# Q of a linear-attention layer computed token by token and turned by the DMA crossbar, its last group computed later, two weights in one buffer

## The chip, the cores and the metric

The kernel runs on one core of a Trainium2 chip. That core has five instruction streams that run side by side and wait for one another by semaphores: PE (TensorE, matmuls; its weight loads are listed as PEld), ACT (ScalarE, activation functions), DVE (VectorE), POOL (GpSimd) and SP (SyncE, which here issues the DMAs). The metric is the device time of one execution in microseconds (us), lower is better. Matmul results go to PSUM, which is cut here into four slots of two banks; everything else lies in SBUF, 128 partitions wide.

## The reference

For x of 2048 tokens by 448 features, two branches work on the same normalised input and are summed with the residual:

```
xn = layernorm(x)
A: q,k,v = xn @ wqkv          16 heads of 28
   pq, pk = q @ w_phi, k @ w_phi (per head)
   phi(p) = [softmax(p), softmax(-p)]          56 features a head
   kv = phi_k^T @ v;  z = sum over tokens of phi_k
   A = ((phi_q @ kv) / (phi_q . z + 1e-6)) @ wo
B: h  = gelu(layernorm(xn) @ w1), its four column blocks shifted by 1, -1, 2, -2 tokens
   x1 = xn + h @ w2
   B  = x1 + gelu(layernorm(x1) @ w3) @ w4
out = x + A + B
```

## The kernel before

Tokens are cut into 16 tiles of 128 (NT), four groups of four tiles. 448 rows of contraction are 3.5 times 128, so nearly every product is done by `pair448` (line 710): two products side by side, each of seven 64-row matmuls, in two halves `.a` (8 matmuls) and `.b` (6); one call is a "pass" of 14 matmuls and takes one PSUM slot. Since the 64-row matmuls run in pairs, a pass costs seven pair steps.

Stages, in the order of data:

- Loads (lines 583 to 637) are issued by SP: x in six pieces, wk, wq, wv and w1, then, after the x transposes, w2 and its copy w2s (lines 1051 to 1056), w3, wo and w4 (lines 1102 to 1104).
- First norm: per tile `st` (statistics), `ag`, `sc` (a power on POOL), `ap` (apply), `du` (lines 762 to 782). xn is then transposed to xnT: tiles 0 to 3 by PE (`xT`, line 794), tiles 4 to 15 each by one DMA transpose on SP, 128x512, `xD4` to `xD15` (line 815).
- w_phi is folded into wk and wq, giving wpk and wpq (`wT`, `fold`, `foldc`, lines 825 to 872).
- `V0` to `V7` (line 890) and `K0` to `K7` (line 908) take a pair of tiles each, tokens on the partitions, 448 columns. K's result is exponentiated twice on ACT (`.e0`, `.e1`), summed per head on DVE (`red`, `rec`) and scaled mostly on POOL (`nrm`).
- `Q0` to `Q7` (line 942) take a group of four tiles and half of the head blocks each: features on the partitions (120), 512 columns of tokens, two exponentials of 120x1024 on ACT straight into eq, which is the stationary operand that `num` needs. Nothing has to be transposed.
- `W10` to `W17` (line 961): w1, with `gel` on ACT (32 instructions), writing each shifted block where it belongs; tiles at the seam go through `nudge` and `put` (lines 980 to 1001). `warm2` loads ACT's gelu table after all exponentials of K and Q.
- `hD0` to `hD7` (line 1002): DMA transposes on SP, 128x1024, of two tiles of h into hT, a ring of three buffers; `W20` to `W27` (line 1061) multiply hT by w2.
- `kv0` to `kv3`, `kvc`, `kvm`, `kvo` (lines 1014 to 1047) make the 56x29 matrix per head.
- Second norm per pair: `W2j.r`, `st2`, `ag2`, `sc2`, `ga`, and `gD` (line 1097), a DMA transpose of g into gT, which has two slots of four tiles.
- `H` (line 1185): w3 and gelu, seven passes of 512 columns a group. `num`, `n1` to `n7`, `od`, `oD` (lines 1110 to 1180): the attention output, normalised on DVE and POOL and transposed on SP. `F` (lines 1214 to 1236): w4 and wo for a pair of tiles, then `fin` on DVE and `out`, one each per tile (lines 1237 to 1247).

What order each engine's instructions have is settled before launch: a list scheduler (class Planner, line 223) starts tasks by a rank and by assumed durations (the third argument of `P.add`), and the table RANKS (line 366) overrides all ranks. Each engine then works strictly in that order, so an instruction that waits holds back all behind it on its engine; on SP that is every DMA issue. Waits are derived from the bytes that instructions touch (class Recorder, line 17), so two uses of one buffer wait for one another. All operations are recorded by helpers: L197 is every matmul, L201 every PE transpose, L205 every ACT instruction, L209 every elementwise one, L212 every plain DMA and L215 every DMA transpose. In the profile's names "eq" is also the buffer in which wk, wq lie at first, "hq" the buffer of h and at first of wpq, "w" any of w1, w2, w3, w4, "wv" also g, "phik" also the H activations, and "xnT<-xnT" is `oD`.

Of the kernel before, what the change touches and what calls it, by code (L numbers as in the profile page):

```python
# [366 lines left out]
warm 868.4 tiny 970.5 phi -70.0 x0 -486.0 x1 -79.6 wk0 -291.7 wk1 284.2 x2 326.9 wv0 1117.1 wv1 954.7 wv2 792.3 wq0  # L367
444.5 wq1 375.6 x4 733.3 x8 1139.7 x12 1546.2 w10 640.0 w11 1288.0 w12 1936.1 bdl -321.6 bdh 970.7@5139 mask
1098.4@1625 pick 966.2@4497 ident 958.1@1998 mhalf -318.4 z_h 959.3@1573 nudge 971.2@1597 z_pk -285.0 z_v -272.1 z_wpq
998.3 z_kvq 286.2 st0 853.0 ag0 208.4 sc0e 294.4 sc0 -285.3 ap0 258.7 du0 57.9 st1 204.5 ag1 60.2@4897 sc1e 288.1 sc1  # L370
997.3 ap1 243.1 du1 1112.4 st2 205.2 ag2 227.0 st3 252.9 ag3 294.2 sc2e 1063.7 sc2 970.7 ap2 63.9 ap3 271.9 du2 268.8
st4 84.4 ag4 239.6 st5 239.8 ag5 874.0 sc4e 102.1 sc4 991.8 ap4 286.4 ap5 495.5 du4 65.4 st6 287.4@11185 ag6 865.4 st7
239.4@11166 ag7 156.1 sc6e 205.0 sc6 971.2@13677 ap6 157.0 ap7 220.7 du6 90.4 st8 28.7@13523 ag8 243.2@16614 st9
288.9@13637 ag9 413.8 sc8e -323.1 sc8 1243.7 ap8 782.0@20130 ap9 797.1 du8 1090.5 st10 243.7@13806 ag10 84.0 st11
259.2@13643 ag11 205.1 sc10e 244.0 sc10 986.2 ap10 495.3 ap11 156.9 du10 82.0@20186 st12 313.5 ag12 204.3 st13 761.4
ag13 28.6@20784 sc12e 263.1 sc12 1162.8 ap12 176.8 ap13 157.2 du12 369.7 st14 234.9@18290 ag14 305.3@19922 st15
82.9@17719 ag15 228.5@19848 sc14e 313.4 sc14 1188.5@22933 ap14 251.2 ap15 262.1 du14 264.6 f0 1188.9 f8 870.9@24467
xT0 296.7@6540 xT1 589.9@8454 xTc0 769.9@7438 xTc1 829.3 xT2 308.9 xT3 575.0 xTc2 822.2@11260 xTc3 896.9@11975 xD4
463.2 xD5 487.3 xD6 397.4 xD7 480.3 xD8 479.7 xD9 456.4 xD10 490.4 xD11 488.2 xD12 476.1@27407 xD13 425.8@25657 xD14
422.8@28403 xD15 486.3@30159 wTk 278.3 wTck0 872.2 wTck1 847.2 foldk0 291.2@8902 foldck0 873.4 foldk1 290.8@7999  # L380
foldck1 861.1 wTq 597.2@7001 wTcq0 815.4 wTcq1 576.6 foldq0 112.7@9432 foldcq0 873.8@10814 foldq1 309.8 foldcq1
770.5@11650 V0.a 131.0 V0.b 596.4 V0.e 814.9 V1.a 611.2 V1.b 621.0 V1.e -217.9 V2.a 283.7@19412 V2.b 243.7 V2.e 855.1
V3.a 258.1@25132 V3.b 615.5 V3.e 530.1 V4.a 413.8 V4.b 487.7@32840 V4.e 648.6 V5.a 2130.9 V5.b 315.3 V5.e 343.8 V6.a
1092.4 V6.b 656.1 V6.e 491.9 V7.a 1096.5 V7.b 374.4 V7.e -228.4 K0.a 590.7 K0.b 596.7 K0.e0 875.6 K0.e1 507.0 red0
1501.6 rec0 1501.9 nrm0 1188.1 red1 1498.0@21181 rec1 118.3 nrm1 1157.5 K1.a 283.9@17349 K1.b 609.8 K1.e0 509.1 K1.e1
-216.6 red2 786.6 rec2 515.2 nrm2 1160.2 red3 264.5@32297 rec3 290.1 nrm3 1159.4 K2.a 575.7 K2.b 283.4 K2.e0
-202.6@23116 K2.e1 919.1 red4 797.0 rec4 226.8 nrm4 870.8 red5 1498.8 rec5 293.5 nrm5 407.5@40914 K3.a 183.0 K3.b
621.3 K3.e0 828.9 K3.e1 501.7 red6 1377.0 rec6 499.7 nrm6 399.9@33939 red7 516.5@30012 rec7 1379.7 nrm7 1187.7 K4.a
675.4 K4.b 1438.8 K4.e0 729.0 K4.e1 718.7 red8 1533.4 rec8 1413.5 nrm8 390.6 red9 1380.6 rec9 1474.4 nrm9 407.3 K5.a
644.7@37806 K5.b 683.8 K5.e0 496.9 K5.e1 496.4 red10 1439.5 rec10 -331.0 nrm10 403.0 red11 1435.2@50122 rec11  # L390
-297.4@53022 nrm11 415.4 K6.a 401.9 K6.b 644.6 K6.e0 -263.9@34806 K6.e1 501.3@33944 red12 1500.3 rec12 1437.9 nrm12
857.2 red13 1417.4 rec13 1380.5 nrm13 1159.5 K7.a 682.7 K7.b 1126.1 K7.e0 493.7 K7.e1 648.4 red14 307.4 rec14 1462.0
nrm14 1098.5 red15 1418.2 rec15 1474.5 nrm15 407.1 Q0.a 569.0 Q0.b 263.5 Q0.e0 543.6 Q0.e1 543.6 Q1.a 290.1 Q1.b 596.6
Q1.e0 785.1 Q1.e1 522.7 Q2.a 1491.2 Q2.b 261.5 Q2.e0 647.5@28961 Q2.e1 242.8@28196 Q3.a 595.2 Q3.b 242.4 Q3.e0 785.4
Q3.e1 -312.2 Q4.a 175.1 Q4.b 283.7 Q4.e0 904.2@33049 Q4.e1 498.8 Q5.a 355.3 Q5.b 413.2 Q5.e0 499.2 Q5.e1 903.8 Q6.a
594.9 Q6.b 478.9 Q6.e0 492.2 Q6.e1 529.8 Q7.a 1057.0 Q7.b 683.2 Q7.e0 349.0 Q7.e1 660.7 warm2 529.2@45117 W10.a
656.5@43897 W10.b 949.8 gel0.0 728.6 gel0.1 340.6 gel1.0 532.8 gel1.1 744.8 W11.a 804.7 W11.b 213.9 gel2.0 -228.0
gel2.1 658.3 gel3.0 482.7 gel3.1 659.0 W12.a 916.6 W12.b 930.6 gel4.0 349.8 gel4.1 494.5 gel5.0 519.7 gel5.1 482.9
W13.a 1439.6 W13.b 682.4 gel6.0 640.8 gel6.1 725.6 gel7.0 492.4@53544 gel7.1 493.3@52599 W14.a 1446.7 W14.b 1478.5
gel8.0 644.4 gel8.1 372.5 gel9.0 349.8@55542 gel9.1 494.5 W15.a 1073.7@51311 W15.b 525.8 gel10.0 658.6 gel10.1 656.9  # L400
gel11.0 349.9 gel11.1 350.4 W16.a 2141.1 W16.b 1086.0 gel12.0 358.7 gel12.1 492.6@57478 gel13.0 688.0 gel13.1
366.6@57534 W17.a 687.1 W17.b 707.4 gel14.0 491.3 gel14.1 492.1 gel15.0 366.1 gel15.1 -228.4 nudge0 1075.4@59991 put8
505.8@60597 put9 327.7@61558 nudge1 1073.1 put7 492.5 put6 736.9 hD0 177.9 hD1 147.9 hD2 187.5 hD3 194.4 hD4 213.9 hD5
223.0@59251 hD6 199.2 hD7 198.0@59683 kv0 918.8 kv1 1477.9 kv2 1071.3 kv3 882.5 kvc 1430.0 kvm 259.3 kvo0 1803.8 kvo1
1544.6 w20 485.1 w21 419.6 w22 417.3 w23 525.4 W20.a 1446.5 W20.b 1060.2 W20.r 1493.4 st2_0 1438.4 ag2_0 1431.6 st2_1
1535.3 ag2_1 1020.8@59199 sc2_0e 1487.3 sc2_0 409.9@61475 ga0 1036.1 ga1 1450.3@62958 gD0 187.6 W21.a 214.3 W21.b
523.9 W21.r 1464.6 st2_2 1438.2 ag2_2 1488.1 st2_3 1437.9 ag2_3 1464.8 sc2_2e 1556.8 sc2_2 376.0 ga2 1418.4 ga3 1036.5
gD1 162.3 W22.a 525.7 W22.b 525.6 W22.r 1557.2 st2_4 1535.7@63878 ag2_4 1826.3 st2_5 1750.8 ag2_5 909.6@73450 sc2_4e
1470.9@74052 sc2_4 947.9@75836 ga4 1547.5 ga5 1503.7 gD2 148.3 W23.a 497.9 W23.b 524.6 W23.r 1849.7 st2_6 1900.8 ag2_6
1451.3 st2_7 1813.2 ag2_7 1410.1@73193 sc2_6e 1487.6 sc2_6 857.8 ga6 1036.7 ga7 749.0 gD3 157.7 W24.a 297.4@76488  # L410
W24.b 525.9 W24.r 1874.5 st2_8 1416.0 ag2_8 1033.4 st2_9 1529.3 ag2_9 1721.7 sc2_8e 1548.2 sc2_8 666.0 ga8 743.9 ga9
1943.6 gD4 266.5@86330 W25.a 907.3 W25.b 279.2@65249 W25.r 1518.3@67862 st2_10 1906.4 ag2_10 1504.1 st2_11
1545.7@73156 ag2_11 1739.6@75171 sc2_10e 1901.7 sc2_10 872.0 ga10 1813.1 ga11 749.7@85280 gD5 290.3 W26.a 1070.4 W26.b
465.7@63251 W26.r 1813.1 st2_12 1567.0@67359 ag2_12 1825.8 st2_13 1036.4@66877 ag2_13 1885.8@74867 sc2_12e 1826.4
sc2_12 407.8 ga12 1828.6 ga13 1545.9@100527 gD6 1700.4 W27.a 283.9@66012 W27.b 297.5 W27.r 1503.5 st2_14 1419.6 ag2_14
1437.5@71900 st2_15 1825.9@74052 ag2_15 1548.0 sc2_14e 1548.2@82777 sc2_14 925.1 ga14 746.9@95166 ga15 1904.0 gD7
1685.8 w30 419.0 w31 406.5 wo0 423.1 wo1 491.3 wo2 461.4 w4 494.1 num0 466.2 n1_0 1546.3 n2_0 1393.7 n3_0 1760.0@76183
n4_0 749.2 n5_0 1904.7 n6_0 1069.2 n7_0 936.0 num1 525.7 n1_1 1544.5 n2_1 1896.2 n3_1 1470.5@81970 n4_1 1559.1 n5_1
1776.2 n6_1 1813.2 n7_1 927.9@86239 od0 1946.5 oD0 268.1 num2 504.3@83674 n1_2 1526.8@85094 n2_2 1770.0 n3_2 1039.2
n4_2 989.8 n5_2 1778.7 n6_2 1814.1 n7_2 1695.3 num3 541.1 n1_3 1796.4 n2_3 1722.5 n3_3 1957.9 n4_3 1527.3 n5_3 1001.0  # L420
n6_3 1526.9 n7_3 662.7 od1 1896.2 oD1 293.4 num4 551.0 n1_4 752.3 n2_4 1546.2 n3_4 1901.0 n4_4 748.0 n5_4 2206.7 n6_4
1533.1 n7_4 1772.9 num5 557.6 n1_5 751.8 n2_5 2205.0 n3_5 1021.6 n4_5 1512.8 n5_5 1021.8 n6_5 1596.5 n7_5 598.4 od2
1015.6 oD2 1674.3 num6 841.7 n1_6 1513.0 n2_6 723.9 n3_6 1593.5 n4_6 745.4 n5_6 1010.2 n6_6 1594.1 n7_6 663.6@106936
num7 1026.4 n1_7 2207.5 n2_7 1545.8 n3_7 1545.5 n4_7 2209.9 n5_7 744.5 n6_7 1542.2 n7_7 600.2 od3 1884.4 oD3 1734.2
# [29 lines left out]
def bass_parallel_sum__linear_kernel_hedgehog__mixer_s_mlp__prompt_kernel(  # L454
# [18 lines left out]
    with es:  # L473
# [62 lines left out]
        for nm, w in (("st", 6), ("mv", 2), ("rs", 2), ("fs", 4), ("st2", 6), ("mv2", 2), ("rs2", 2)):  # L536
            stat[nm] = new(nm, NT * w, F32).rearrange("p (t c) -> p t c", t=NT)
# [423 lines left out]
        for j in range(8):  # L961
# [5 lines left out]
            for d, i in enumerate((i0, i1)):  # L967
                for q in range(2):
# [7 lines left out]
                    for m in (2 * q, 2 * q + 1):  # L976
                        made[i, m] = g_
# [304 lines left out]
```

The softmax here doesn't subtract the row's maximum and nothing guards it: scores larger than these inputs give would overflow.

## Time and profile before

| | |
|---|---|
| time, median of 3 runs | 177.67 us (177.43 to 177.85) |
| the profiled execution | 177.84 us, its span 176.1 us |
| granted TensorE clock | 1.000 |
| longest idle of PE after its start | 0.93, 0.53, 0.43, 0.32 us |
| last matmul group starts, by the PE timeline | 172.82 us, `F7_1.b` |
| ACT_TABLE_LOAD | 2 of 1283 ns |
| exponential 128x896 (K), mean | 954 ns, x16 |
| exponential 120x1024 (Q), mean | 1061 ns, x16 |
| DMA transposes, issue to landing | xnT 2.5, hT 3.3, gT 3.3, oT 3.1 us |

The share of busy time is an average over stages. A PE that is shown as busy nearly all the time says that whatever is taken off PE's stream can shorten the kernel, and that whatever makes PE wait lengthens it; it does not say that the work is the least there could be. Durations of matmuls in a list are from issue to end and overlap: two neighbours of 349 ns start 0.19 us after the pair before. Cost is therefore read from the starts of groups in the timeline.

### The profile page before, as it was taken

What the parts mean: (1) busy time and instruction counts of PE and PEld (TensorE: products, weight loads), DVE (VectorE), ACT (ScalarE), POOL (GpSimd) and SP (SyncE); (2) the same over time, 40 slices, a digit from 0 to 9 for tenths busy, and PEclk for the clock granted to TensorE, in tenths of its full rate; (3) what the DMA queues carried; (4) which work ended last, traced back from release to release, by engine and by line L of the source; (5) the groups of instructions that cost most, each with busy time, mean ns of one, the idle gap of its engine ahead of it and who ended that gap; (6) DMA issues with size and microseconds to landing.
All of it is one profiled execution on the core that took longest, in us unless ns stands there. A gap on an engine that the chain in (4) does not pass through costs nothing.

```text
span 176.1 us, 4846 instructions
## 1 busy us (share of the span) xinstructions
PE 169.2 (96%) x2080; PEld 111.4 (63%) x2080; DVE 116.4 (66%) x300; ACT 81.4 (46%) x116; POOL 77.8 (44%) x105
## 2 busy tenths in 40 slices
PE   5999999999999979999999999999999999999993
PEld 4766566676666665455555667655676666766793
DVE  3879999977995798995986655830654554370133
ACT  3398999999999510264557100327001561200000
POOL 7515578699339334035432253640037141261080
PEclk9999999999999999999999999999999999999999
DMA  6993444599918496625054616130010403313022
GB/s 146 279 339 83 72 83 91 101 360 327 331 49 162 77 122 123 119 32 93 0 98 86 120 27 149 53 63 0 0 56 26 89 0 63 60 52 63 0 86 78
DMA packets 41766, 18.30 MB, mean 104 GB/s; under 512 B 33552, under 2 KB 40848, under 8 KB 41744
## 3 DMA queue, kind: packets, MB, share of 16 engines
q1 hardware_dynamic: 41136, 17.91, 43.2%
q8 instruction: 16, 0.26, 0.6%
q10 hardware_dynamic: 608, 0.08, 0.3%
q14 instruction: 6, 0.05, 0.1%
HBM read 8.28 MB, written 1.84 MB: 57 GB/s over the span
## 4 chain that ended last, share of the span: by engine, by line
PE 86%; DMA 8%; SPq 3%; issue 1%; DVE 0%; DVEq 0%
PE ps L197 86%; DMA wv<-in_A_wqkv_dram 4%; SPq L212 3%; DMA hT<-hq 3%; DMA gT<-wv 2%; DVE vaug L209 0%; DVEq L169 0%; SPq L215 0%
## 5 line engine op out<-in xcount | busy, mean ns | idle before, releaser
L205 ACT ACTIVATE phik<-ps 128x1024 bf16<-128x1024 f32 (+1 forms) x44 | 41.3, 997 | 45.4 <-PE ps L197 45.4
L209 DVE TENSOR_TENSOR vaug<-ps,vaug 128x464 f32<-128x464 f32 (+3 forms) x66 | 32.8, 505 | 21.3 <-PE ps L197 15.9
L197 PE MATMUL ps<-w,phik 64*128 64x448 bf16 (+1 forms) x504 | 45.9, 328 | 0.0
L197 PE MATMUL ps<-gT,w 64*128 64x512 bf16 x392 | 44.5, 376 | 0.3 <-DMA gT<-wv 0.3
L197 PEld LDWEIGHTS ps<-w,phik 64*128 64x128 bf16 x504 | 29.5, 94 | 12.3 <-ACT phik L205 0.3
L197 PEld LDWEIGHTS ps<-gT,w 64*128 64x128 bf16 x392 | 23.0, 94 | 17.4 <-DVE vaug L209 0.7
L209 POOL TENSOR_TENSOR xnT<-vaug 128x224 bf16<-128x224 f32 x32 | 17.3, 564 | 27.7 <-DVE vaug L209 27.7
L209 POOL TENSOR_TENSOR vaug<-xn,xtok 128x448 f32<-128x448 bf16 x16 | 16.4, 1037 | 28.5 <-DVE vaug L209 26.4
L209 POOL TENSOR_TENSOR phik<-phik,ksum 128x896 bf16<-128x896 bf16 x14 | 24.1, 1749 | 8.2 <-DVE ksum L209 8.2
L209 POOL TENSOR_TENSOR rs<-rs,mhalf 128x2 f32<-128x2 f32 (+1 forms) x17 | 11.5, 683 | 28.3 <-DVE rs L209 22.0
L205 ACT ACTIVATE eq<-ps 120x1024 bf16<-120x1024 f32 (+1 forms) x18 | 17.5, 1045 | 6.1 <-PE ps L201 4.9
L209 DVE TENSOR_REDUCE ksum<-phik 128x32 f32<-128x896 bf16 x16 | 16.6, 1059 | 1.1 <-ACT phik L205 1.0
L209 DVE RECIPROCAL vaug<-ps 128x16 f32<-128x16 f32 x16 | 4.1, 254 | 19.1 <-PE ps L197 19.1
L197 PE MATMUL ps<-wo,xnT 64*128 64x448 bf16 (+1 forms) x126 | 14.1, 328 | 0.0
L197 PE MATMUL ps<-wv,xnT 64*128 64x448 bf16 x112 | 13.6, 349 | 0.5 <-DMA wv<-in_A_wqkv_dram 0.5
L197 PE MATMUL ps<-xnT,hq 64*120 64x512 bf16 x112 | 13.6, 377 | 0.0
L197 PE MATMUL ps<-wpk,xnT 64*128 64x448 bf16 x112 | 13.2, 349 | 0.0
L197 PE MATMUL ps<-w,hT 64*128 64x448 bf16 x56 | 12.1, 349 | 0.9 <-DMA hT<-hq 0.9
L197 PE MATMUL ps<-w2s,hT 64*128 64x448 bf16 x56 | 12.1, 350 | 0.0
L209 DVE BATCH_NORM_STATS2 st<-xtok 128x6 f32<-128x448 bf16 x16 | 9.2, 614 | 3.2 <-DMA xtok<-in_A_x_dram 3.2
L197 PE MATMUL ps<-w,xnT 64*128 64x448 bf16 x112 | 11.2, 349 | 0.0
L205 ACT ACTIVATE hq<-ps,fs 128x224 bf16<-128x224 f32 x32 | 11.0, 493 | 0.2
(71 smaller groups left out, 174.5 us busy)
## 6 DMA issues: line engine op xcount, KB each, us to landing
w<-in_B_w_dram SPq DMA_DIRECT2D x2, 896.0 KB, 7.0
w<-in_B_w_dram SPq DMA_DIRECT2D x1, 1568.0 KB, 12.3
out_dram<-vaug SPq DMA_DIRECT2D x14, 112.0 KB, 1.7
xtok<-in_A_x_dram SPq DMA_DIRECT2D x3, 448.0 KB, 7.0
eq<-in_A_wqkv_dram SPq DMA_DIRECT2D x2, 336.0 KB, 3.7
w<-in_B_w_dram SPq DMA_DIRECT2D x2, 336.0 KB, 7.3
wv<-in_A_wqkv_dram SPq DMA_DIRECT2D x1, 336.0 KB, 6.5
w2s<-in_B_w_dram SPq DMA_DIRECT2D x1, 336.0 KB, 5.4
```

The lines of the kernel that those rows point to most:

```text
L197: self.op("PE", lambda e: e.matmul(out, lhsT, rhs, start=start, stop=stop, skip_group_check=True), [out], [lhsT, rhs], after=after)
L205: self.op("ACT", lambda e: e.activation(out, in_, func, **kw), [out], [in_] + aps)
L209: self.op(eng, lambda e: getattr(e, name)(out, *args, **kw), [out], aps)
L212: self.op(eng, lambda e: e.dma_start(out, in_), [out], [in_], dma=True)
```

## The change

Q of token tiles 0 to 11 becomes six passes `Q0` to `Q5` like K's: a pair of tiles, tokens on the partitions, 448 columns. Their exponentials (128x896) are written head by head with a gap of 8 in 64 into phiq (two buffers), and one DMA transpose for each pair, 128x2048, `qD0` to `qD5`, moves it to eq, whose layout becomes tile, sign, block, token. phiq lies in gT's bytes, so every write of gT waits for all qD. Q of tiles 12 to 15 stays as it was (two passes of 512 columns, now `QL6` and `QL7`), but stands among the W2 passes; ACT loads the exp table before them (`warm3`) and the gelu table again behind them (`warm4`). wo and wpk are one buffer, so the load of wo waits for all K passes. wpq gets a buffer of its own.

In the same diff: g of the second pair (tiles 2, 3) is transposed by eight PE transposes and two copies in place of `gD1`; `fin` and `out` handle two tiles in one instruction; the clearing of the buffer that the 20 start-up matmuls read is split so that they need half of it; the assumed load rates change; and all of RANKS is replaced by new values, so the order on every engine is new.

```diff
-        wpq = view(hq_r, 4 * 512).rearrange("p (b c d) -> p b c d", b=4, c=NC)
+        wpq = new("wpq", 4 * 512).rearrange("p (b c d) -> p b c d", b=4, c=NC)
...
-        eq = view(eq_r, NG * NC * 2 * 512).rearrange("p (g c s f) -> p g c s f", g=NG, c=NC, s=2)
+        eq = view(eq_r, NT * 2 * 512).rearrange("p (t s c n) -> p t s c n", t=NT, s=2, c=NC)
...
+        wpk_r = region("wpk", 4 * D * 2)
+        wpk, wo = (view(wpk_r, 4 * D).rearrange("p (c d) -> p c d", c=4) for _ in range(2))
...
+        gT_r = region("gT", 2 * 4 * 512 * 2)
+        gT = view(gT_r, 2 * 4 * 512).rearrange("p (b t c n) -> p b t c n", b=2, t=4, c=4)
+        phiq = view(gT_r, 2 * 2048).rearrange("p (b t h d) -> p b t h d", b=2, t=2, h=16)
...
+        LATE_Q = (6, 7)
+
+        def q_tiles(j):
+            i0, i1 = 2 * j, 2 * j + 1
...
+            mq_ = lambda p, k: wpq[p, k, :, :].rearrange("p c (u d) -> p (c u) d", u=2)[:, :, 0:56]
+            ta, tb = pair448(nm, rk, xT(i0, i1) + fold_done["q"], D, tok(xnT, i0), mq_, tok(xnT, i1), mq_, [key])
...
+                    R.act(phiq[:, P.slot[key], :, 8 * s:8 * s + 8, 0:56],
+                          both(P.slot[("ps", nm)])[:, :, 0:D].rearrange("p t (h d) -> p t h d", d=56), ACT.Exp, scale=1.0 - 2.0 * s)
...
+            def mvq(t, i0=i0, key=key):
+                R.dmaT(eq[:, i0:i0 + 2, :, :, :].rearrange("p t s c n -> p (t s c) n"),
+                       phiq[:, P.slot[key], :, :, :].rearrange("p t h d -> p (t h d)"))
+            q_ready[j] = [P.add("qD%d" % j, "SP", TI, rk, ex + fold_done["k"], mvq, [key], lag=3000)]
+            q_moved.extend(q_ready[j])
...
+        lq_act = []
+        warm3 = P.add("warm3", "ACT", 1400, 128, w1_act, lambda t: R.act(tiny[:, 0:1], tiny[:, 1:2], ACT.Exp))
+        for n in LATE_Q:
+            q_features(n, warm3, lq_pe, lq_act)
+        warm4 = P.add("warm4", "ACT", 1400, 140, lq_act,
+                      lambda t: R.act(tiny[:, 0:1], tiny[:, 1:2], ACT.Gelu_apprx_tanh))
...
+        G_PE, G_ACT = (1,), ()
...
+                            R.tr(v[:, 128 * c:128 * c + 128], g_tok[:, P.slot[("g", j)], d, 128 * c:128 * c + 128], ident[:, :])
+                tt = P.add("gP%d" % j, "PE", 8 * 56, G_RANK[j], ga + [t_id], gtr, gk + [k2], mode=128)
...
-            g_ready[i0] = g_ready[i1] = P.add("gD%d" % j, "SP", TI, G_RANK[j], ga, gd, gk, lag=TL2)
+            g_ready[i0] = g_ready[i1] = P.add("gD%d" % j, "SP", TI, G_RANK[j], ga + q_moved, gd, gk, lag=TL2)
...
-        l_wo = load_dup("wo", wo, A_wo, 92, "SP", None, late)
+        l_wo = load_dup("wo", wo, A_wo, 92, "SP", None, late + k_pe)
...
-                            R.mm(b[:, at_:at_ + 60], eq[p, g, c, s, 128 * jj:128 * jj + 128], kvq[p, s, c, :], True, True)
-            tn = P.add("num%d" % i, "PE", 238, NUM_RANK[i], q_ready[g] + kv_dma, num, [k] + ring, mode=64)
+                            R.mm(b[:, at_:at_ + 60], eq[p, i, s, c, :], kvq[p, s, c, :], True, True)
+            tn = P.add("num%d" % i, "PE", 238, NUM_RANK[i], q_ready[i // 2] + kv_dma, num, [k] + ring, mode=64)
...
+                    def fin(t, k=k, i0=i0, i1=i1, u=u, v=v, rows=rows):
+                        R.ew(dve, "tensor_tensor", rows(outb, "ob"), both(P.slot[k])[:, :, 0:v - u], rows(xs, "xs"), op=ALU.add)
```

The order of issue on SP from the first DMA transpose to the first `gD`, in both kernels:

```
before: xD4..xD15 | w3, w2s, w3, w2, wo, wo, w2, wo, w4, w2s | hD0..hD5 | gD0
after:  xD4, xD5, qD0, xD6, qD1, xD7..xD11, qD2, xD12, xD13, qD3, xD14, xD15
        | w4, w3, w3, w2, qD4, w2, w2s, w2s, wo, wo, qD5, wo | hD0..hD5 | gD0
```

On PE, by the new order: `Q0`, `Q1`, then V, K and `Q2` to `Q5` mixed, the eight W1 passes, `kv0`, `nudge0`, `kv1`, `nudge1`, then `W20`, `W21`, and `QL6`, `W22`, `kv2`, `QL7`, `W23`, `W24`, `kv3`, `gP1`, `W25`, `kvm` mixed, then H of groups 0 and 1 with `num0` to `num5`, `W26` and `W27`, and from there F and H as before.

## The prediction

> **What bounds the kernel now.** I read the page's busy shares first, then the chain of waits, then the timelines of PE and SP, and last the DMA view of the stretch that the change moves.
>
> ```profile
> PE 169.2 (96%) x2080; PEld 111.4 (63%) x2080; DVE 116.4 (66%) x300; ACT 81.4 (46%) x116; POOL 77.8 (44%) x105
> ```
>
> PE is busy 169.2 of 176.1 us. The chain of waits, in order of time, shows where it isn't:
>
> ```profile
> 13.43 16.05 PE ps L197 x160
> 29.48 0.04 issue
> 29.52 29.50 PE ps L197 x302
> 59.02 4.92 DMA hT<-hq
> 63.94 0.14 issue
> 64.08 5.09 PE ps L197 x92
> 69.17 0.05 SPq L215
> 69.22 0.04 issue
> 69.26 3.31 DMA gT<-wv
> 72.57 0.25 issue
> 72.82 100.50 PE ps L197 x1262
> ```
>
> From 13.43 us on the chain is PE, except for two DMA transposes, hT and gT, and there PE lost only 0.93 and 0.32 us. After 72.82 PE never waits. So two things count: PE's work, and the arrival of hT and gT between 56 and 73 us. PE's price list comes from its timeline:
>
> ```profile
> 15.31 3.20 PE L197 MATMUL ps<-xnT,hq 64*120 64x512 bf16 x28
> 18.34 0.94 PE L197 MATMUL ps<-wv,xnT 64*128 64x448 bf16 x8
> ...
> 46.93 9.46 PE L197 MATMUL ps<-w,xnT 64*128 64x448 bf16 x98
> 56.20 0.35 PE L197 MATMUL ps<-w,hT 64*128 64x448 bf16 x1
> ```
>
> 28 matmuls of 512 columns fill 15.31 to 18.34: 0.216 us a pair, 1.515 a pass. 98 of 448 columns fill 46.93 to 56.20: 0.189 a pair, 1.32 a pass. Now SP, in the same stretch:
>
> ```profile
> 32.12 1.27 SPq L215 DMA_TRANSPOSE xnT<-xn  x1
> 33.44 0.58 SPq L212 DMA_DIRECT2D w<-in_B_w_dram  x1
> ...
> 38.59 0.60 SPq L212 DMA_DIRECT2D w<-in_B_w_dram  x1
> 39.24 6.35 SPq L212 DMA_DIRECT2D w2s<-in_B_w_dram  x1
> 52.35 2.64 SPq L215 DMA_TRANSPOSE hT<-hq  x2
> ```
>
> The late weights (w2, w2s, wo, w3, w4) start right behind the last x transpose, at 33.44; their last issue hangs for 6.35 us. The busy time by stretch tells when they are through (DMA share and GB/s are the last two columns), and the DMA issues of that stretch how long they took to land:
>
> ```profile
> 48.00:49.00 1.00, 1.00 (x14) 0.64 (x11) 1.00 (x2) 0.85 (x4) 0.76 (x1) 1.00 0.97 294
> 49.00:50.00 1.00, 1.00 (x15) 0.66 (x12) 1.00 (x2) 1.00 (x4) 0.00 (x0) 1.00 0.20 53
> ```
>
> ```profile
> w<-in_B_w_dram SPq DMA_DIRECT2D x1, 1568.0 KB, 12.3
> ...
> w2s<-in_B_w_dram SPq DMA_DIRECT2D x1, 56.0 KB, 11.8
> ```
>
> The DMA engines are full until about 49.2: 15.8 us after the first issue. 56 KB, issued last, took 11.8 us, as long as the 1568 KB ahead of it. The first hT transpose is issued at 52.35, 3 us after the engines had emptied.
>
> **What the skill says.** The Trainium skill, "DMA: Bandwidth & Descriptors", section "Queues, rings and completion order", says that SP's DMAs share one row of rings over the same 16 DMA engines and that each engine takes descriptors in ring order; the 11.8 us of the 56 KB agree. The same page, "Latency and other measured facts", gives a DMA transpose 261 GB/s, or 350 to 400 when contiguous. The trace is slower: from 52 to 60 us hT transposes alone moved 98 GB/s at a DMA share of 0.51, 192 GB/s when full. "ScalarE: Activation LUTs", "What ACT_TABLE_LOAD costs", says about 1283 ns; the two in the trace average 1283.
>
> **The change part by part.**
>
> Q's work. Eight passes of 1.515 (12.1 us) become six of 1.32 and two of 1.515 (10.95): PE saves 1.2. `gP1` adds eight transposes, 0.54 us as the eight of xn at 11.42, plus one change of matmul mode, 0.6 together. ACT saves more, four 120x1024 exponentials less in the first stage and 12 that step at 0.83 in place of 0.94 us (six of K's fill 4.96 us), so it no longer paces that stage: ACT needs 27.4 us there (16 of K, 12 of Q, 5 of V at 0.83), PE 26.4 after the first two passes.
>
> Start. wq comes as SP's fifth load and wk later, against wk second before; the copies of x transposes and folded weights on ACT (0.6 and 0.87 us each) follow one another either way. I put two finished passes at 15.4 us, where before has them at 15.31; 0.7 us either way is not excluded, since the clearing is shorter (a gain) and two folds now stand between Q's passes (a loss of up to 0.9).
>
> PE's own arrival at W2. From 15.4: 20 passes of K, V and Q at 1.32 are 26.4 (41.8), eight of W1 10.6 (52.4), two kv and two nudges 2.4 (54.8). Those kv need the scaled K tiles: POOL's 12 at about 1.7 us from about 27 us on are done by 48, hidden.
>
> From W2 to the end. Before's 72.82 to 173.32, 100.5 us, holds H, F, 15 num and one W2 pass. Add seven W2 passes (9.3), `num0` (0.24), QL (3.03), kv2 and kv3 (2.0), gP1 (0.6), kvm (0.35): 116.0. A wait at `gP1`: DVE must do three residual sums (1.08 each), six statistics (0.57 each) and small steps before the second pair's `ga`; I find it 0.5 late. 116.5. The sum of before's passes from 15.31 to 72.82 misses 0.76 us of switching; half of it goes on each side of W2's start. The two extra table loads, 1.5 each with their dummy, lie on ACT between the gelus' end (about 56) and H's first gelu (about 70): nothing, unless QL is over 3 us late. The later store, merged, is one 128x448 sum in place of two 128x224 ones and one DMA of the same bytes: nothing.
>
> So with nothing new to wait for PE ends at 54.8 + 116.5 + 0.76 = 172.06, against 173.32: 1.26 us less.
>
> hT's arrival. This is where I expect the change to lose. SP now issues 16 transposes, not 12, before the late weights. At 1.27 us each (the median of xnT's) from 15.3 that ends at 35.6, at before's pace (18.06 us for 12) at 39.4; I take 36.5. The weights are the same bytes: 15.8 us, to 52.3. `qD4` and `qD5` stand among them. A 128x2048 transpose isn't in the trace; 512 KB take 2.7 us at the measured 192 GB/s, 1.3 at the page's 400. I take 2.2 each (an estimate): 56.7. `hD0` becomes issuable early, 3.85 us after the first gelu (48.50 to 52.35 before; gelus now start near 44.5, so near 48.3), but it is behind all of that in the rings, and needs its own 256 KB, 1.4 us: it lands at 58.1. PE is at W2 by 55.2 with half of the switching, and in its fixed order nothing else may go first: `QL6` stands behind `W21`. It waits some 3 us, and W2, the second norm, gT and H shift with it. End: 58.1 + 116.5 + 0.4 = 175.0, 1.7 later than 173.3. The later hD3 to hD5 follow freed buffers and stay ahead.
>
> The shared wo/wpk buffer makes SP wait at wo for the last K pass, at about 41; the rings are full then: nothing. gT's wait for all qD ends ten us before its first use: nothing.
>
> **The sum.** The profiled execution took 177.84 for a last PE step ending at 173.3; 1.7 more is 179.5. It lies 0.17 above the median of the runs shown, so 179.4 for the median.
>
> **Rivals.**
>
> 1. hT isn't held up. For it: W2 could wait at most if PE is really early, and the backlog may drain faster: 35.6 + 15.8 + 2.6 + 1.4 = 55.4 puts hT level with PE. Against it: every term must be at its low end. Then the time is 177.67 - 1.26 = 176.4. The point from which it decides: hT before 56.4 us makes the kernel faster, after it slower.
> 2. The two cancel: hT at 56.1 to 56.9. Time 177.6.
> 3. The transposes of 128x2048 hold SP nearly as long as their transfer. For it: 16 queued transposes load the engines more than xnT's 0.42. Against it: issue hardly grows with size (1267 ns for 128x512, 1302 for 128x1024). Four times 0.6 us puts the weights at 39 and hT at 60.5: 177.4, so 181.7; x tiles 6 and 7 would also reach K late, but inside that wait.
>
> **How the numbers follow.** A change under 0.2% (0.36 us) can't be told from none here. hT held up as worked out: 0.52, 179.4, own range 178.0 to 181.0. Rival 3: 0.14. Rival 1: 0.26. Rival 2: 0.08. Faster 0.26, same 0.08, slower 0.66. The range needs both signs: down to 176.0, just under rival 1's 176.4 for the start's 0.7, and up to 182.2, over rival 3; beyond it lie hT at 62.0 (39.4 + 15.8 + 5.4 + 1.4, 183.2) and a start that gains all of its 0.7 with no wait.
>
> **What would show it.** Right: PE idle for some 3 us before the first matmul on hT, released by the DMA of hT; that DMA 8 us or more from issue to landing; a DMA share near 1 until 56 us; Q's passes at 0.189 us a pair. Wrong: hT landing 4 us after issue with PE waiting less than 1 us; the weights issued by 35 us; or PE idle in the first stage on xnT, or after H's start, of which this sum has none.

## The result, and the profile after

The changed kernel took 190.06 us (median of four runs, 189.66 to 191.76), the kernel before 177.76 us beside it: a ratio of 1.072 (1.063 to 1.080). The profiled execution took 190.28 us with a span of 188.2, 12.1 more than before's 176.1. The forecast was right that it is slower and that PE would wait on hT at W2; the loss is seven times the 1.7 us forecast. In all ratios here, executions more than 1.5% above the fastest of the same kernel are left out.

PE's row of busy shares and the granted clock, from the page of the kernel after:

```profile
PE 171.6 (91%) x2088; PEld 107.4 (57%) x2088; DVE 114.8 (61%) x291; ACT 85.9 (46%) x124; POOL 76.1 (40%) x105
...
PEclk9999999999999559999999999999999999999999
```

PE is busy 2.4 us longer and the span is 12.1 us longer, so PE stands idle where it didn't before; and two slices of the clock say 5. The chain of waits says where (start, length, what):

```profile
22.91 4.82 DMA xnT<-xn
...
43.52 15.64 PE ps L197 x205
...
63.12 3.41 DMA hT<-hq
...
66.67 13.71 PE ps L197 x156
...
80.82 104.39 PE ps L197 x1304
```

Before, the chain was PE from 13.43 us on but for hT and gT. Now a DMA of xnT carries it in the first stage, hT carries it to 66.67, and only from there on is it PE to the end. (Ahead of hT the chain names ScalarE's table load as what released `qD5`'s issue on SP. That is inferred, and the experiment with w4 and wo behind hD5 speaks against it: there `qD5`'s issue ends at 55.6 and this table load starts at 60.4.) PE's timeline has the lengths (in square brackets the idle time before the group, and what ended it):

```profile
27.77 0.93 PE L197 MATMUL ps<-wpk,xnT 64*128 64x448 bf16 x7 [1.99 <-DMA xnT<-xn]
...
43.52 0.93 PE L197 MATMUL ps<-wpk,xnT 64*128 64x448 bf16 x7 [0.82 <-DMA xnT<-xn]
...
45.99 10.94 PE L197 MATMUL ps<-w,xnT 64*128 64x448 bf16 x112
...
66.67 0.53 PE L197 MATMUL ps<-w,hT 64*128 64x448 bf16 x1 [7.52 <-DMA hT<-hq]
```

W1 starts at 45.99, which the prediction had at 41.8. After it PE finishes at 59.15 all that it may do before W2, and waits 7.52 us. SP's timeline of the same time tells why hT comes then:

```profile
42.29 3.83 SPq L212 DMA_DIRECT2D w<-in_B_w_dram  x4
46.16 9.96 SPq L215 DMA_TRANSPOSE eq<-gT  x1
...
59.14 3.30 SPq L215 DMA_TRANSPOSE eq<-gT  x1
...
63.12 12.76 SPq L215 DMA_TRANSPOSE hT<-hq  x6
```

The late weights start at 42.29 (before: 33.44). `qD4`, the fifth transpose of Q, is next and its issue hangs for 9.96 us; everything behind it in SP's queue, `hD0` too, waits with it. The hold ends when the DMA engines have nearly run dry (the last two columns are their busy share and GB/s):

```profile
53.00:54.00 1.00, 1.00 (x14) 0.56 (x12) 0.06 (x1) 1.00 (x5) 0.00 (x0) 1.00 1.07 381
...
55.00:56.00 1.00, 1.00 (x14) 0.51 (x10) 0.00 (x0) 1.00 (x5) 0.00 (x0) 1.00 0.55 32
```

`hD0` is issued at 63.12 and, by the chain, lands 3.41 us later. Its data had been ready for some 10 us: with the same order on ScalarE it is issued at 52.7 in one of the experiments. Last, the busy time by stretch across PE's wait (the third column from the right is the granted clock):

```profile
61.00:62.00 1.00, 0.00 (x0) 0.00 (x0) 0.00 (x0) 0.99 (x2) 0.00 (x0) 0.55 1.24 279
...
69.00:70.00 1.00, 1.00 (x9) 0.41 (x7) 0.00 (x0) 0.00 (x0) 0.00 (x0) 0.50 0.08 9
...
71.00:72.00 1.00, 1.00 (x10) 0.61 (x8) 1.00 (x1) 0.00 (x0) 0.00 (x0) 0.83 0.00 0
```

The clock falls to half at 61.1 us, 1.9 us after PE has run out of work, and comes back at 71.3. `W20` and `W21`, 14 pair steps, take from 66.67 to 71.60: 4.93 us where 14 times 0.189 are 2.65. The half clock costs 2.3 us beyond the wait.

From W2 on nothing else is lost: 66.67 to 185.22 are 118.55 us, less 2.28 for the clock 116.3; the prediction had 116.5.

So the 12 us are made before W2 ends, by three things: SP's queue in the first stage, SP's queue ahead of `hD0`, and the clock. Theory A is that the six 128x2048 transposes do all of it, by their time on SP and in the DMA rings. Rival B is that the new order of all instructions loses by itself. Theory C is that the clock falls because PE stands idle. In all experiments below "PE's wait" is idle time of PE in that kernel's profiled execution.

### The profile page after: what moved, and what is told of

Read it like the earlier page. It is cut to its first block, busy times and chain, and to the rows that moved or that the text cites. A ratio compares the mean times of both kernels' runs of the same rounds, so it can differ in the third digit from the quotient of the medians.

```text
span 188.2 us, 4863 instructions
## 1 busy us (share of the span) xinstructions
PE 171.6 (91%) x2088; PEld 107.4 (57%) x2088; DVE 114.8 (61%) x291; ACT 85.9 (46%) x124; POOL 76.1 (40%) x105
## 4 chain that ended last, share of the span: by engine, by line
PE 81%; DMA 9%; ACT 4%; SPq 3%; DVE 1%; issue 1%
PE ps L197 80%; DMA xnT<-xn 4%; DMA eq<-in_A_wqkv_dram 3%; SPq L212 2%; DMA hT<-hq 2%; ACT phik L205 2%; PE ps L201 1%; ACT vaug L205 1%; SPq L215 1%; ACT L205 1%; DVE ksum L209 1%; ACT hq L205 0%; DVE vaug L209 0%; DVE hq L209 0%; ACT tiny L205 0%
## 5 line engine op out<-in xcount | busy, mean ns | idle before, releaser
L197 PE MATMUL ps<-wpk,xnT 64*128 64x448 bf16 (+1 forms) x238 | 29.2, 338 | 2.8 <-DMA xnT<-xn 2.8
L209 POOL TENSOR_TENSOR rs<-rs,mhalf 128x2 f32<-128x2 f32 (+1 forms) x17 | 11.6, 688 | 44.8 <-DVE rs L209 44.8
L209 POOL TENSOR_TENSOR phik<-phik,ksum 128x896 bf16<-128x896 bf16 x13 | 21.7, 1702 | 0.7 <-DVE ksum L209 0.7
L197 PE MATMUL ps<-w,hT 64*128 64x448 bf16 x56 | 14.2, 399 | 7.5 <-DMA hT<-hq 7.5
L197 PEld LDWEIGHTS ps<-wpk,xnT 64*128 64x128 bf16 x238 | 14.1, 94 | 11.5 <-DMA xnT<-xn 3.5
L209 DVE TENSOR_TENSOR xn<-ps,xn 128x896 bf16<-128x896 f32 x8 | 8.5, 1072 | 11.7 <-PE ps L197 11.7
L205 ACT ACTIVATE eq<-ps 120x1024 bf16<-120x1024 f32 (+1 forms) x6 | 5.7, 992 | 19.7 <-PE ps L197 14.1
L197 PE MATMUL ps<-w2s,hT 64*128 64x448 bf16 x56 | 14.2, 400 | 0.0
L197 PEld LDWEIGHTS ps<-w,hT 64*128 64x128 bf16 x56 | 5.6, 105 | 10.9 <-issue 9.0
L197 PE MATMUL ps<-wpq,xnT 64*128 64x448 bf16 x84 | 11.2, 350 | 0.0
L205 ACT ACTIVATE gT<-ps 128x896 bf16<-128x896 f32 (+1 forms) x13 | 11.0, 903 | 0.1
```

The costliest lines, as they stand in the source:

```text
L197: self.op("PE", lambda e: e.matmul(out, lhsT, rhs, start=start, stop=stop, skip_group_check=True), [out], [lhsT, rhs], after=after)
L205: self.op("ACT", lambda e: e.activation(out, in_, func, **kw), [out], [in_] + aps)
L209: self.op(eng, lambda e: getattr(e, name)(out, *args, **kw), [out], aps)
```

## The experiments

Where a DMA is said to be moved, the order that the planner had made is kept as it is and only that DMA is moved in SP's queue.

| kernel | ratio to before (95%) | weights' first issue | hD0 issued | W2 starts | PE's wait on xnT / hT |
|---|---|---|---|---|---|
| before | 1 | 33.44 | 52.35 | 56.20 | 0 / 0.9 |
| after | 1.072 (1.063, 1.080) | 42.29 | 63.12 | 66.67 | 2.8 / 7.5 |
| Q as features, planned anew | 1.158 (1.153, 1.163) | 49.09 | 60.20 | 71.81 | 2.9 / 2.5 |
| Q copied, not transposed | 1.022 (1.018, 1.027) | 39.04 | 54.60 | 60.61 | 0 / 0 |
| w4, wo behind hD5 | 1.034 (1.027, 1.041) | 41.36 | 55.63 | 59.10 | 1.0 / 0.5 |
| products in PE's wait | 1.063 (1.057, 1.068) | 41.34 | 64.51 | 68.02 | 1.6 / 3.0 |
| qD4, qD5 behind hD5 | 1.039 (1.035, 1.043) | 41.68 | 52.71 | 59.81 | 1.4 / 1.1 |
| w4, wo behind gD3 | 1.019 (1.013, 1.025) | 42.85 | 56.12 | 60.36 | 0.9 / 0.4 |
| ... and a longer start | 1.032 (1.028, 1.036) | 40.69 | 54.54 | 57.90 | 0.7 / 2.3 |
| ... and qD0, qD1 later | 1.029 (1.027, 1.031) | 42.25 | 55.79 | 61.72 | 2.5 / 0 |
| before + 6 transposes | 1.060 (1.056, 1.064) | 41.05 | 59.84 | 66.24 | 6.1 / 3.2 |
| before + the last 2 | 1.011 (1.006, 1.015) | 33.24 | 52.22 | 57.69 | 0 / 0.9 |
| before + the first 4 | 1.041 (1.038, 1.045) | 41.28 | 60.06 | 63.93 | 4.2 / 0.9 |
| before, w4, wo behind gD3 | 1.036 (1.032, 1.040) | 32.95 | 52.04 | 55.93 | 0 / 0.9 |

**Q as features, without the transposes.**

```diff
             if j not in LATE_Q:
-                q_tiles(j)
+                q_features(j, warm, kq_pe, kq_act)
```

> Q of the first three groups is computed feature-major on PE and ScalarE, straight into eq, so that the six 128x2048 transposes are not issued at all; the last group stays late, and everything else keeps its rank. Theory A (the six transposes hold SP and fill the DMA rings: xnT late in the first stage, the late weights late, hD0 stuck behind qD4's issue): no wait on xnT over 0.5 us in the first stage, the late weights issued at about 36 instead of 42.3, no issue on SP over 4 us, PE's wait on hT at most 2 us instead of 7.5, PE at full clock through W2; PE pays 6 x 0.19 us for the feature-major passes. Sum 190.1 - (about 3 + 6 + 2.3) + 1.2 = 178 to 181. Rival B (the new order of the instructions loses by itself, transposes or not): the first stage and the arrival at W2 stay as they are and the time stays above 187. The planner lays the stage of W2 and H out anew here, so the part up to the start of W2 counts most.

Measured: 205.69 us (204.7 to 206.48). This experiment failed. With other durations and dependencies the planner made another order: the twelve transposes of xn alone spread from 14.89 to 49.09, the weights behind them start at 49.09, and the largest wait, 6.8 us on VectorE's g, is in the second norm. It speaks neither for A nor against it; the later kernels keep the planned order for that reason.

**The same bytes, copied instead of transposed.**

```diff
-                R.dmaT(eq[:, i0:i0 + 2, :, :, :].rearrange("p t s c n -> p (t s c) n"),
-                       phiq[:, P.slot[key], :, :, :].rearrange("p t h d -> p (t h d)"))
+                R.dma(eq[:, i0:i0 + 2, :, :, :].rearrange("p t s c n -> p (t s c n)"),
+                      phiq[:, P.slot[key], :, :, :].rearrange("p t h d -> p (t h d)"))
```

> Each 128x2048 transpose of Q is replaced by a plain copy of the same 0.52 MB from the same tile into the same part of eq, at the same place of SP's queue; the pad columns are set to 1 instead of 0. Q's features then lie in eq untransposed, so the output is not the reference's; every instruction after it runs as before on other values. Theory A1 (it is the kind of the transfer: 256-byte packets at about 170 GB/s, 3.1 us for 0.52 MB): the copies go at the 360 to 400 GB/s that the bulk weights show here, 1.4 us each, 10 us of ring time less in all; hD0 is issued some 5 to 7 us earlier, PE's wait on hT falls to 1 to 3 us, the clock stays up; 180 to 184. Theory A2 (the bytes alone, or the issue's own time on SP): hardly any change, 188 to 190.

Measured: 181.94 us (180.21 to 182.1). SP's timeline of this kernel:

```profile
39.04 3.81 SPq L212 DMA_DIRECT2D w<-in_B_w_dram  x4
43.47 0.47 SPq L212 DMA_DIRECT2D eq<-gT  x1
...
54.60 13.07 SPq L215 DMA_TRANSPOSE hT<-hq  x6
```

At the place where `qD4`'s issue hung for 9.96 us the copy's takes 0.47, and `hD0` is issued at 54.60. Both xnT waits and the hT wait are gone; the first stage has another wait instead, 1.7 us on DVE. 8.1 of the 12 us go with the kind of the transfer alone; order, bytes and SP's number of issues are the same. So "the bytes alone" falls, and rival B can have no more than the 4 us that are left. How these divide isn't shown. In this execution the clock was half from 9.3 to 16.1, and the first two passes of Q were done at 18.96 instead of 16.12. But the bytes still count too:

```profile
hT<-hq SPq DMA_TRANSPOSE x1, 5.9
```

`hD0`, issued at 54.60, took 5.9 us to land, to 60.5, and PE came to W2 at 60.61. Had PE started 2.8 us sooner, it could have waited here for most of that time.

**w4 and wo behind hD5.**

```diff
-        l_wo = load_dup("wo", wo, A_wo, 92, "SP", None, late + k_pe)
+        l_wo = load_dup("wo", wo, A_wo, 92, "SP", None, late + k_pe + [hT_ready[5]])
-        l_w4 = [load("w4", ..., 94, "SP", 1568, late)]
+        l_w4 = [load("w4", ..., 94, "SP", 1568, late + [hT_ready[5]])]
```

> The loads of w4 and wo are made to follow hD5; w3 and w2 stay ahead of it, and all six transposes of Q stay. Theory A (hD0 is late because qD4's issue stands behind rings full of weights): the first stage keeps its two xnT waits and PE comes to W2 at about 59, but 2.4 MB of w4 no longer stand ahead of qD4, qD5 and hD0; hD0 is issued at about 53 to 56 instead of 63.1, PE's wait on hT is 0 to 1.5 us instead of 7.5 and its clock does not fall; 190.1 - 7.5 - 2.3 + (0 to 1.5) = 180 to 182. Rival (the transposes by themselves keep the rings full, wherever the weights stand): hD0 comes 1 to 2 us earlier at most, 187 to 189. If w4 comes too late for the last product, that shows as a wait on w4 there.

Measured: 184.07 us (182.51 to 186.59), 2 to 4 more than expected. The two loads are 1568 and 448 KB, 2.0 MB together, where the expectation gave w4 2.4. The hT part is right: `hD0` at 55.63, PE's wait 0.5 us. But w4 is now issued just ahead of the first transpose of g:

```profile
66.78 0.58 SPq L212 DMA_DIRECT2D w<-in_B_w_dram  x1
68.59 2.94 SPq L215 DMA_TRANSPOSE gT<-wv  x1
```

That transpose's issue holds SP 2.94 us; H's first product waits 2.4 us, and the clock is half from 76.2 to 79.6. The loss moved to the next transpose behind the same bytes.

**Products in PE's wait, to hold the clock.**

```diff
+            if n == 1:
+                def filler(t):
+                    for _ in range(36):
+                        R.mm(bank(P.slot[("ps", "filler")], 0)[:, 0:D], ident[:, :], w1[:, 0, :], True, True)
+                P.add("filler", "PE", 10, -1e6, [tn, t_id] + l_w1, filler, [("ps", "filler")], mode=128)
```

> 36 products of 448 columns that nobody reads are added on PE behind the second nudge, in what is PE's wait on hT (about 6.8 us of work in 7.5 us of wait); everything else, SP's queue too, keeps its order. Theory C (PE's idle time lets the granted clock fall to half for some 8 us, which costs the first two passes of W2 some 2.3 us beyond the wait itself): the clock stays at 0.9 or more through W2, W20 and W21 take 2.7 instead of 4.9 us, and the time is 187.6 to 188.2. Rival (the fall of the clock has another cause, or costs nothing because the passes wait on something else anyhow): 189.7 to 190.5.

Measured: 190.41 us (187.93 to 191.63). By the ratios, 1.063 against 1.072 with intervals that overlap, a gain isn't clear. In the profiled execution PE worked on them until 65.1, but `hD0` was issued at 64.51 this time, so 2.6 us of wait were left, and the clock was half from 69.4 to 72.8. Of the four executions three had a mean clock of 0.989 to 0.991 and took 189.45 to 191.63; one had 0.999 and took 187.93 (the changed kernel's four: 0.963 to 0.973). Only in that one did the clock stay up, as theory C asks, and it shows the expected gain; one execution, which has no trace, is support, not proof.

**The six transposes put into the kernel before.** Nothing else changes there; each turns a part of x into gT, which is empty at that time.

```diff
+        at_of = dict(zip(("xD5", "xD6", "xD11", "xD13", "w20", "wo1"), range(6)))
+        # behind each of these, on SP:
+        R.dmaT(gT[:, n % 2, :, :, :].rearrange("p t c n -> p (t c) n"),
+               xtok[:, 0:5, :].rearrange("p t d -> p (t d)")[:, 0:2048])
```

> The kernel before, with nothing changed but six 128x2048 crossbar transposes added to SP's queue at the places where the change has its six (behind the second, third, eighth and tenth transpose of xn, and two among the late weights); they turn a part of x that lies in SBUF anyway into gT, which is empty then, and nobody reads what they wrote. Theory A (the transposes, by their time in the rings and on SP, are the loss): xnT becomes late in the first stage (1 to 4 us of waits on PE), the late weights start 5 to 6 us later, one issue holds SP for 6 to 10 us, hD0 is issued 6 to 12 us later, PE waits 4 to 8 us on hT and its clock falls; 177.7 + 8 to 12 = 186 to 190. Rival B (the new order and the late group are what loses, and the kernel before would bear the transposes): at most 3 us more, 178 to 181.

Measured: 188.15 us (187.63 to 188.6), 10.5 above before. No engine reads these transposes' data, no other engine's order differs, and they reproduce most of the change's 12 us. PE's timeline:

```profile
28.35 1.67 PE L197 MATMUL ps<-wpk,xnT 64*128 64x448 bf16 x7 [4.54 <-DMA xnT<-xn]
...
40.06 0.93 PE L197 MATMUL ps<-wpk,xnT 64*128 64x448 bf16 x8 [1.54 <-DMA xnT<-xn]
...
66.24 0.35 PE L197 MATMUL ps<-w,hT 64*128 64x448 bf16 x1 [2.36 <-DMA hT<-hq]
```

In before's order of the x transposes the four places in the first stage are behind the second, third, fifth and ninth of them (the expectation counted them in the changed kernel's order). Here the larger part, 6.1 us and a stretch of half clock behind it, is lost on xnT, and hT costs less than in the changed kernel: one issue among the weights hangs for 7.62 us, but `hD0` at 59.84 waits for its gelus, which come late themselves. The same transposes hit the wait that the order puts first.

**The last two of them alone, and the first four alone.** The same edit with `n > 3`, and with `n < 4`.

> As the kernel before with six added transposes, but only the last two of them, the ones among the late weights. Theory A: no xnT waits and the late weights start on time, but the two transposes are queued behind full rings and hold SP; with 17 us of bulk from 36.5 and twice 3 us for the transposes hD0 lands some 5 to 7 us later than before, where it had 3 to 4 us to spare: PE waits 2 to 4 us, 180 to 183. If the loss of the six is mainly made in the first stage (the start of the weights pushed from 36.5 to 42): 177.5 to 179.

> The kernel before with only the first four of the six added transposes, those among the transposes of xn. With all six it lost 10.5 us, with the last two alone 1.8. Theory A (SP and the rings are one line: what the first four take there is paid by xnT in the first stage, 6.1 us of waits with six, and what the last two take is paid by hT only in so far as the weights already start late): the two xnT waits stay at 5 to 6 us together, the late weights start at about 41 instead of 33.4, but without the last two among them hD0 is issued when its gelus are done and PE waits less than 1.5 us on hT: 184 to 185.5. If the loss of six is more than the sum of its parts (the weights' late start alone makes hT late): 186 to 188.

Measured: the last two 1.011 (1.006 to 1.015) of before, that is 179.5 us (the median of all four is 180.89); the first four 185.09 us (184.48 to 185.46). The first four came out as expected but for xnT, 4.2 us of wait where 5 to 6 were expected. The last two met neither of their cases: the time is above the second one's 177.5 to 179, and PE's wait on hT stayed at 0.9 us, where the first had 2 to 4. They hold SP 7.56 and 2.85 us from 37.59 on and still let `hD0` go at 52.22, since the weights had started at 33.24. The first four push the weights from 33.44 to 41.28, 2.0 us each; their own issues are 2.18, 1.39, 1.86 and 1.40 of that. By the ratios the parts, 1.1% and 4.1%, make 5.2 of the 6.0%.

**qD4 and qD5 behind hD5**, in the changed kernel.

```diff
+        move(["qD4", "qD5"], "hD5")
```

> The changed kernel with the last two transposes of Q moved on SP from among the late weights to behind hD5; all weights stay ahead of hD0, every other engine keeps its order. Theory A, as far as qD4's issue is what holds hD0: hD0 now stands where qD4 stood, behind rings full of 4.4 MB of weights, so it is itself held until about 56 and not until 63.1; its data come at about 59.5, PE's wait on hT falls from 7.5 to 0 to 1.5 us and the clock stays up there. But the first transpose of g stands behind qD4 and qD5 (and gT may only be written when they are done), so the hidden layer's first product waits 3 to 6 us at about 73: 184 to 187. If the rings alone (the number of bytes ahead of hD0) count and not the queue of SP, hD0 still lands as late as 62 to 65: 188 to 190.

Measured: 184.76 us (183.83 to 185.03). SP's timeline:

```profile
49.09 2.27 SPq L212 DMA_DIRECT2D wpk<-in_A_wo_dram  x3
52.71 14.13 SPq L215 DMA_TRANSPOSE hT<-hq  x6
66.88 5.78 SPq L215 DMA_TRANSPOSE eq<-gT  x2
```

All late weights (4592 KB) stand ahead of `hD0`, and it still goes at 52.71, nearly as in the kernel before: the plain loads took their places in the rings in 10 us, from 41.68 to 51.4. Now `hD0` is the first transpose behind them, and its own issue and landing are longer:

```profile
52.71 3.44 SPq L215 DMA_TRANSPOSE hT<-hq  x1
```

```profile
hT<-hq SPq DMA_TRANSPOSE x1, 7.0
```

It lands at 59.7. So the bytes in the rings do delay it, as the prediction said, but they are not what kept its issue until 63; that is the transpose that stood between. The expectation had a longer hold, to about 56. What is left is of the kind expected: the first transpose of g has to wait for both, and H's first product waits 2.4 us, less than the 3 to 6 expected.

**w4 and wo behind gD3**, in the changed kernel, with the six transposes where they were.

```diff
+        move(["w4", "wo0", "wo1", "wo2"], "gD3")
```

> The changed kernel with w4 and wo moved on SP to behind the transposes of the first two groups of g; w3, w2, w2s and all of Q's transposes stay ahead of hD0. Theory A: PE comes to W2 at about 59 as before this edit (the two xnT waits of the first stage stay, 1 to 3 us), the wait on hT is at most 1 us, and the wait of the hidden layer's first product on gT, which w4 ahead of the first transpose of g caused (2.4 us and a fall of the clock), goes as well: 190.1 - 7.5 - 2.3 = 180 to 181.5. What is left above the kernel before is then the first stage. If w4 and wo now come too late, PE waits on them at the first product with w4, at about 95.

Measured: 180.76 us (180.2 to 182.23), as expected. Moving four loads takes back 9 of the 12 us. `qD4` is still held, but less and earlier:

```profile
44.50 6.93 SPq L215 DMA_TRANSPOSE eq<-gT  x1
...
56.12 11.70 SPq L215 DMA_TRANSPOSE hT<-hq  x6
```

PE's waits after the start are 0.9 us on xnT, 0.5 on DVE and 0.4 on hT. In this execution the clock was half from 8.4 to 15.3, behind an idle gap of 1.9 us.

**A longer start, and Q's first two transposes later.** Both are made on top of the last kernel.

```diff
-                R.mm(bank(P.slot[("ps", "spin")], 0)[:, 0:240], z[:, 0:128], z[:, 0:240], True, True)
+                for _ in range(1 if n < SPIN - 1 else 15):
+                    R.mm(bank(P.slot[("ps", "spin")], 0)[:, 0:240], z[:, 0:128], z[:, 0:240], True, True)
```
```diff
+        move(["qD0"], "xD7")
+        move(["qD1"], "xD9")
```

> The kernel with w4 and wo behind the transposes of g, and 14 more of the products at the very start that nobody reads (1.4 us of work in PE's wait of 1.1 to 1.9 us on the first weights). Clock theory: in the run with w4 and wo late the granted clock was half from about 9.3 to 16 us, after PE had stood idle from 5.6 to 7.6, and the first two passes of Q were finished 2.5 us later than in the changed kernel's profiled run; kept busy through that gap PE keeps its clock, Q's passes are finished at 16.0 to 16.5, the times scatter by less than 1 us, and the median falls from 180.8 to 178.5 to 179.5. Rival (the fall at the start comes from something else, or the products only delay the first transposes of the weights): 180.3 to 181.5, with the same scatter.

> As the kernel with the longer start, and Q's first two transposes moved on SP behind the fourth and the sixth transpose of xn instead of behind the second and the third. Theory A (in the first stage SP and the rings serve 12 transposes of xn and 4 of Q one after the other, and what stands ahead is paid by xnT): the wait on xnT near 28 us (0.9 to 2 us) goes, unless ScalarE now waits for phiq's first buffer, which Q's third pair needs at about 25 us: 0.5 to 1.5 us less than without this edit, 177.5 to 178.7, level with the kernel before (177.7). Rival (the sum of the transposes' time is what counts and the wait only moves to a later tile): no change against the kernel with the longer start.

Measured: 183.54 us (181.36 to 185.59) and 182.74 (182.2 to 185.05). Neither gained. The first did what it was meant to in its profiled execution, the fastest of its six: full clock throughout, Q's first passes done at 16.19, W2 begun at 57.90, 2.5 us sooner than without. But SP gained only 1.6 us (`hD0` at 54.54 for 56.12), and PE waited 2.3 us on hT. Two further executions at a mean clock of 1.0 took 182.51 and 183.27; why they are slower than the 180.2 to 180.9 of the kernel without the longer start isn't explained by any trace here. The second moved a wait, as its rival said:

```profile
32.23 2.31 PE L197 MATMUL ps<-wv,xnT 64*128 64x448 bf16 x22 [1.16 <-ACT gT L205]
...
39.89 1.38 PE L197 MATMUL ps<-wv,xnT 64*128 64x448 bf16 x7 [2.52 <-DMA xnT<-xn]
```

The wait near 28 us is gone; ScalarE's hold on phiq costs 1.16 us and a later tile of xnT 2.52. So this change of order gained nothing, which fits that the sum of the transposes on SP counts.

**The kernel before with w4 and wo behind gD3**, a try to beat both.

```diff
+        move(["w4", "wo0", "wo1", "wo2"], "gD3")
```

> A try at a kernel faster than both: the kernel before with w4 and wo moved on SP behind the transposes of the first two groups of g, nothing else. There PE waits 0.9 us on hT near 64 us and 0.3 us on gT near 72. If these waits come from weights still in the rings: 176.4 to 177.2. If they come from the time that each transpose of h holds SP (six took 11.0 us, after the weights had landed): no change, 177.0 to 177.5; if w4 then stands ahead of the later transposes of g and delays them: 178 to 180.

Measured: 184.35 us (182.89 to 187.54). The 0.9 us wait on hT stays without w4 and wo in the rings, so these didn't cause it; it goes with the six issues of hT, 11.6 us on SP. What was lost is the edit's place: in before's order `gD3` comes ahead of `gD2`, so w4 and wo now stand ahead of the transpose that the second group's H needs.

```profile
79.28 3.28 SPq L212 DMA_DIRECT2D wo<-in_A_wo_dram  x3
82.61 9.86 SPq L215 DMA_TRANSPOSE gT<-wv  x3
```

The first of these three is `gD2`; it takes 6.0 us from issue to landing (median 3.6), to 88.6, and PE stands idle from 84.95 to 88.71. It is one more transpose made late by bulk ahead of it. No version that I ran beats the kernel before.

Together the runs show that the transposes make most of the loss: 8.1 of the 12 us go when they are copies, and they alone cost the kernel before 10.5. That they make all of it, as theory A has it, isn't shown, and theory C rests on one execution.

## Why the prediction was wrong

- **The work of PE: right.** 14 matmuls of Q take 1.32 us, W2 to the end 116.3 us without the clock's share (116.5 forecast), and the merged store, the shared wo and wpk buffer and `gP1` show no wait after W2. ACT's table loads, four of 1.28 us, are not among PE's waits.
- **The start: 0.7 us late**, at the edge of the bound given. Two passes were done at 16.12, not 15.4.
- **PE's own arrival at W2: wrong.** The sum said 55.2, with "PE idle in the first stage on xnT, or after H's start, of which this sum has none" as a sign that it is wrong. The sign came: xnT made PE wait twice, 2.8 us, and PE was through at 59.15. The step that failed is the one that put the x transposes' lateness only on the weights.
- **The weights' first issue: mis-sized.** 36.5 with bounds of 35.6 and 39.4 became 42.29. The term was 1.27 us for an issue of any size, from 128x512 and 128x1024. The 128x2048 issues took 1.39 at least and up to 3.59 us in the first stage, and four of them cost 2.0 us each in the kernel before, because they also slow the others. Rival 3 named this mechanism, with 39 for the weights.
- **hT's arrival: the mechanism named was not the one that decided.** The sum had `hD0` issued near 48.3 and then queued in the rings behind 20 us of transfers; 58.1. It was not issued before 63.12, because `qD4`, which got 2.2 us of ring time and nothing for SP, held SP itself for 9.96. The prediction's own lines had a warning: the last of the plain loads, 56 KB at 39.24, hangs for 6.35 us behind the same bulk. PE's wait became 7.5 us in place of 3. That `qD4` is the holder is shown from three sides: copied, it lets `hD0` go at 54.6; moved behind, at 52.7; with w4 not ahead of it, at 55.6 and 56.1. The Trainium skill, "DMA: Bandwidth & Descriptors", section "Queues, rings and completion order", gave the prediction the order in the rings, and that holds here: with `qD4` and `qD5` behind hD5 the weights start at 41.68, and the prediction's 15.8 for them and 1.4 for `hD0` give 58.9, where it landed at 59.7. The step went wrong by taking SP as free to issue. Whether the transpose holds SP because its own descriptors find no room or for another reason was not tried.
- **The clock: missing.** No term stood for it, and the profile of before didn't show it (its granted clock was 1.000); among later executions of before there are two at 0.981, which took 180.5 and 180.8 us. It cost 2.3 us here. The Trainium skill, "TensorE: Matmul & The Clock Gate", "Part 1: The HAM clock gate", has a free-running activity window of about 3.4 us; the stretches of half clock agree to the tenth: 10.2 us in the changed kernel, 3.4 with w4 and wo behind hD5 and with the added products, 6.8 at the start of the kernel with copies and of that with w4 and wo behind gD3. The same section's table has half the clock follow at least one such window of idleness; here it fell 1.9 us into a wait, so the table's condition doesn't hold in this trace.

In all: PE's last matmul ended at 185.2, where 175.0 was forecast. Of these 10.2 us the start has 0.7, the first stage's waits and gaps 3.2, the longer wait on hT 4.6 (7.5 for the forecast 2.9), the clock 2.3, and the rest came out 0.6 shorter. The sign stood, and so did the place of the largest wait. The mechanism stood only in part: hT was late, but by SP's hold and not by the order in the rings alone. Two terms were bounded from neighbours of another size; xnT's waits and the clock had no term.

## What to carry to other kernels

Before moving work from an engine into a DMA transpose, add up the issue times of its queue, not only the bytes: a transpose issued behind bulk loads can hold its queue until they have nearly drained, and everything behind it, however small and ready, waits too. A plain load can as well: the last of ten held SP for 6.35 us in the kernel before. Put bulk that is needed late behind the transposes, but look at which transpose comes next behind it. When PE is about to wait for more than a microsecond or two, price a chance of half the clock for the work that follows.

## What was not expected of the hardware

- A 128x2048 transpose among bulk loads held SP's issue for 9.96 us (6.2 to 9.1 us in the other kernels with it there); a plain copy of the same bytes at the same place took 0.47 us, and four plain loads together 3.83. The copy's own landing was hardly sooner (10.5 us after the issue, 12.0 for the transpose); what it spared is SP.
- No length of gap decides alone. Idle gaps of PE of 1.2 and 1.9 us (at the start), 2.4 (at H), 2.5 (xnT) and 2.6 (hT) were followed by half the clock, each time for a whole multiple of 3.4 us. Others of 1.9 and 2.0 us, of 2.4 at H with `qD4` and `qD5` moved and of 2.9 on xnT with Q as features were not. All five of 3.7 us and more were. So the same program can scatter: the changed kernel over 2.1 us, that with w4 and wo behind hD5 over 4.1, the kernel before over 0.9 in eleven executions of one set and over 3.7 in eleven of another.
